# RWKV attention and gated MLP on one core: joint transposing DMAs, and a new order of the work

## The chip, the cores and the metric

The kernel runs on one core of a Trainium2 chip. The metric is device time in microseconds, the median of repeated executions. The engines in the text are TensorE (PE; its weight loads are shown as PEld), VectorE (DVE), ScalarE (ACT), GpSimd (POOL) and SyncE (SP), which issues most of the DMAs. Each runs its own instructions in order and waits for the others through semaphores. A DMA that SP issues is carried out by 16 DMA engines, which all queues share.

## The reference

Inputs r, k, v have shape (4, 8, 768, 48): batch, heads, time, head size. A recurrence over time with a decay w and a bonus u per head gives y; y, with its heads side by side, is the 3072 x 384 input of an MLP with 2048 hidden units and a smooth gate.

```python
for t in range(S):
    cur = einsum('bhd,bhe->bhde', u * k[t], v[t])
    y[t] = einsum('bhd,bhde->bhe', r[t], state + cur)
    state = w * state + einsum('bhd,bhe->bhde', k[t], v[t])
x = y.transpose(0, 2, 1, 3).reshape(B * S, H * D)
h = x @ w_in
g = where(h >= 1, h, where(h <= -1, 0, (h + 1) ** 2 / 4))
out = g @ w_out
```

## The kernel before

The time axis is cut into 6 chunks of 128 steps. A *unit* is one chunk of one batch entry (128 tokens, 8 heads), numbered n; a *group* g is two units, so there are 24 units in 12 groups. Names below are those of the code and, shortened, of the profile.

For each group SP loads R, K and V (L364, L438): 384 KB each, group 0's R and K in two halves. R is scaled by powers of the decay into Rs (L383) and K into Ks (L385), in bf16 and padded from 48 to 64 columns a head. KU = K times u (L387), RKU = R times KU (L389), its sums over a head `diag` (L411), and V2 = V times diag (L416), the bonus term. These products run on GpSimd; in the first three groups (`FLEX`) they may run on VectorE.

Attention of a unit needs scaled R and K turned, so that the head's 48 columns lie on partitions. For groups 0 to 4 (`TDMA` = 5) TensorE turns them: T, eight matmuls against an identity matrix (L462), then a copy TT from PSUM to SBUF by ScalarE or VectorE (L248). From group 5 on SP issues two transposing DMAs per group (L546), one into RT and one into KT. Then come A (L473), its masked copy AT on VectorE (L478), Y from the state and from AT times V (L495, L500), and y = Y + V2 (L507). Sp (L485), Tm (L515), the decay of the state on GpSimd (L520) and its bf16 copy `state_bf` carry the recurrence to the next chunk.

For the MLP y must be turned as well. In groups 0 to 2 (`XDMA` = 3) TensorE does it (X, L528) with a copy to xT; from group 3 on SP issues one transposing DMA per unit (L569), which writes the unit's half of the group's tile xT. mm1 (L602) is four blocks of 12 matmuls with 256 columns per group (in group 0 in halves of 128 columns). Its result passes ScalarE twice (relu L610, square L615) and VectorE once (gate, L620), then mm2 (L651), four blocks of 4 matmuls per unit. The output is copied from PSUM and stored by SP (L666).

The weights are loaded by GpSimd's queue, four transfers of w_in (L320) and four of w_out (L326); the first of each waits for a load of R or K (L314). While the MLP of group 0 has not filled PSUM, gaps on TensorE are filled with identity matmuls, named `warm` (L679).

The order of all this is set by a planner in the kernel. Each operation is declared with `op`: the engines that may run it, with a cost and a delay to its result, a key, what it needs, and the tile slots it takes and frees. A loop then picks, again and again, the operation that can start earliest by these costs (within 0.25 us, the lowest key), and emits it. The table `TUNE` adds an amount to the key by kind and group ('m' is groups 4 to 9), and `ONLY` fixes an operation that has two engines to one of them (0 is the first named). For the products of the first groups 0 is GpSimd and 1 is VectorE; for TT, o and xT 0 is ScalarE and 1 is VectorE. So a changed cost, a changed key and a changed slot count all change the order of every engine's instructions, SP's queue among them. The number of identity matmuls in a gap is worked out from the planner's own idea of how long TensorE will be free.

Of the kernel before, what the change touches and what calls it, by code (L numbers as in the profile page):

```python
# [10 lines left out]
BF16 = mybir.dt.bfloat16  # L11
# [12 lines left out]
def kernel(  # L24
# [86 lines left out]
    Rs = [const.tile([P, UNITS * H, HP], BF16, name="Rs", tag=f"Rs{i}") for i in range(NB)]  # L111
    Ks = [const.tile([P, UNITS * H, HP], BF16, name="Ks", tag=f"Ks{i}") for i in range(NB)]
    for i in range(NB):
        nc.vector.memset(Rs[i][:, :, D:], 0.0)
        nc.vector.memset(Ks[i][:, :, D:], 0.0)
# [31 lines left out]
    FLEX, XDMA, TDMA, VCAST = 3, 3, 5, 12  # L147

    def shift(what, g):
# [17 lines left out]
        'Wdn': {0: -9.14},  # L167
        'Wup': {0: 1.93},
        'X': {0: 0.79, 1: -2.24, 2: -4.04},
        'Y': {0: -0.05, 3: 3.62, 10: 0.23, 11: -1.39, 'm': -2.74},  # L170
        'decay': {2: 0.48, 3: -11.42, 'm': -2.78},
        'exps': {0: 7.52},
        'gate': {0: 20.08, 1: 8.66, 2: -1.81, 3: -14.22, 10: 0.46, 'm': -3.69},
        'load': {0: -2.22, 1: 2.92, 2: 1.11, 11: 5.77, 'm': 11.7},
        'lw': {0: 3.06},
        'lw_row': {0: -3.75},
# [6 lines left out]
        'u_bc': {0: 6.26},  # L183
        'u_row': {'m': -2.41},
        'usum': {0: -0.67, 1: 19.78, 2: 1.23, 3: -1.67, 10: -0.52, 11: 1.53, 'm': -1.65},
        'wCm': {0: 9.26},
        'w_in': {0: -0.2, 1: -1.68, 2: -0.05, 3: 2.64},
        'w_in!': {0: -5.6, 1: 36.74, 2: 2.76, 3: -7.13},
        'w_out': {0: 0.06, 1: -8.78, 2: 4.51, 3: -1.32},
        'w_out!': {1: -0.28, 2: -2.83, 3: 4.56},  # L190
        'w_power': {0: 0.75},
        'w_row': {0: 3.3},
        'w_take': {0: 5.37},
        'wc': {0: 5.72},
        'xT': {0: 9.53, 1: -3.07, 2: 0.34, 3: -1.67, 10: 0.36, 11: 5.32, 'm': -2.7},
        'y': {0: -3.24, 1: 0.72, 2: 1.77, 3: -1.94, 10: -14.8, 11: 4.13, 'm': -3.61},
# [97 lines left out]
    op("w_row", (("NET", 0.0, 3.4),), -99, None)  # L294
    op("u_row4", (("NET", 0.0, 4.4),), -99, None)
    op("lw_row", (("ACT", 0.52, 0.05),), -98, lw_ln, ["w_row"])
    op("lw", (("PE", 1.3, 0.17),), -98, lw_mm, ["lw_row"], [("bank", "lw")], ["lw"])
    op("wc", (("PE", 0.6, 0.17),), -99, w_mm, ["w_row"], [("bank", "wc")], ["wc"])
# [4 lines left out]
    op("w_take", (("DVE", 0.15, 0.08),), -95, w_take, ["wc"], [], ["wc"])  # L303
# [7 lines left out]
    for i in range(max(NW, NO)):  # L311
# [23 lines left out]
        k_in = -70 + i  # L335
        k_out = -1 + i * 0.1 + shift("w_out", i)
        op(f"w_in{i}!", (("POOL", 0.78 + 0.2 * (i in GATE_IN), 1.5),), k_in, w_in_go, after(GATE_IN, i, "w_in"), [], [GATE_IN[i][:2]] if i in GATE_IN else [])
        op(f"w_in{i}", (("SWD", 2.5, 1.35),), k_in, None, [f"w_in{i}!"])
        op(f"w_out{i}!", (("POOL", 0.78 + 0.2 * (i in GATE_OUT), 1.5),), k_out, w_out_go, after(GATE_OUT, i, "w_out"), [], [GATE_OUT[i][:2]] if i in GATE_OUT else [])
        op(f"w_out{i}", (("SWD", 10.6 / NO, 1.35),), k_out, None, [f"w_out{i}!"])  # L340

# [463 lines left out]
```

## Time and profile before

| | |
|---|---|
| median of 3 runs | 183.79 us (183.52 to 184.97) |
| profiled execution | 183.7 us |
| its span in the profile | 181.9 us |
| mean granted TensorE clock | 1.0 |
| matmuls | 1850, of them 182 identity matmuls `warm`, 80 of T, 18 of X |
| transposing DMAs | 32: 18 of y, 7 of R, 7 of K |
| moved by DMA | 27.75 MB, mean 153 GB/s |

The span is shorter than the device time because launch and end lie around it. The profile gives, for each engine, the busy time and its share of the span; groups of instructions by line with their mean duration; a timeline of instructions with start, duration and, in brackets, the idle time before and what ended it; a list of waits; and tables by stretch of time. A line `34.17 2.78 PE L602 MATMUL ... x24` means that 24 matmuls of line 602 began at 34.17 us and the last of them ended 2.78 us later. Matmuls overlap in the pipeline, so the distance from one start to the next says more of their cost than the mean duration does.

### The profile page before, as it was taken

How to read it: one execution, taken by the hardware profiler on the slowest of the kernel's cores; microseconds unless marked ns; L12 is line 12 of the kernel's file. 1: busy time of each engine (PE TensorE's matmuls, PEld its weight loads, DVE VectorE, ACT ScalarE, POOL GpSimd, SP SyncE). 2: the span in 40 equal slices, each digit the busy share in tenths (PEclk: the TensorE clock that was granted, in tenths of full speed). 3: DMA queues.
4: the chain of work that ended last, by engine and by line, in shares of the span. 5: the costliest groups of instructions: out<-in, count | busy, mean ns of one | idle time of the engine just before them, and what ended most of it. 6: DMA issues, size and time to landing. Idle time of an engine off the chain costs nothing.

```text
span 181.9 us, 4539 instructions
## 1 busy us (share of the span) xinstructions
PE 171.7 (94%) x1850; PEld 129.7 (71%) x1850; DVE 140.2 (77%) x207; ACT 133.8 (74%) x169; POOL 111.6 (61%) x88
## 2 busy tenths in 40 slices
PE   5999999969999999999998999999899999999992
PEld 4897888747778787587876677767667777777761
DVE  6977499599998879789986888768687998754360
ACT  5455896678767978668986987786977798774762
POOL 2793553029999998979939949898859551000000
PEclk9999999999999999999999999999999999999999
DMA  6999999999997599998989999889798822101032
GB/s 123 189 214 188 212 199 186 176 208 182 193 192 162 96 218 196 141 215 180 147 151 168 178 200 183 162 179 206 142 183 108 193 83 65 22 4 43 0 130 86
DMA packets 103806, 27.75 MB, mean 153 GB/s; under 512 B 97125, under 2 KB 103786, under 8 KB 103786
## 3 DMA queue, kind: packets, MB, share of 16 engines
q1 hardware_dynamic: 100064, 24.32, 75.5%
q0 software_dynamic: 3712, 3.15, 10.7%
q8 instruction: 14, 0.23, 0.6%
q14 instruction: 6, 0.05, 0.1%
q10 hardware_dynamic: 10, 0.01, 0.0%
HBM read 20.45 MB, written 4.72 MB: 138 GB/s over the span
## 4 chain that ended last, share of the span: by engine, by line
PE 41%; DMA 17%; POOL 14%; SPq 13%; DVE 7%; issue 3%; ACT 3%; DVEq 0%; ACTq 0%; POOLq 0%
PE op L651 18%; PE hp L602 17%; DMA K<-in_k_dram 14%; SPq L364 8%; POOL RKU L389 4%; POOL state L520 3%; DVE gt L620 3%; POOL Ks L385 3%; SPq L438 3%; POOL KU L387 3%; DMA R<-in_r_dram 3%; PE A L473 2%; ACT sq L615 2%; SPq L546 1%; PE T L462 1%
## 5 line engine op out<-in xcount | busy, mean ns | idle before, releaser
L620 DVE SCALAR_TENSOR_TENSOR gt<-sq,hp 128x1024 bf16<-128x1024 f32 (+1 forms) x52 | 58.7, 1134 | 25.5 <-ACT sq L615 25.1
L602 PE MATMUL hp<-xT,w_in_sb 128*128 128x256 bf16 (+1 forms) x624 | 71.7, 264 | 1.8 <-DVE gt L620 1.0
L651 PE MATMUL op<-w_out_sb,gt 128*128 128x384 bf16 x384 | 72.3, 326 | 0.1
L602 PEld LDWEIGHTS <-w_in_sb 128*128 128x128 bf16 x624 | 57.1, 98 | 14.1 <-issue 3.4
L610 ACT ACTIVATE pt<-hp 128x1024 f32<-128x1024 f32 (+1 forms) x52 | 49.6, 954 | 23.5 <-PE hp L602 23.4
L615 ACT ACTIVATE sq<-pt 128x1024 f32<-128x1024 f32 (+1 forms) x52 | 51.6, 992 | 1.1
L651 PEld LDWEIGHTS <-gt 128*128 128x128 bf16 x384 | 34.6, 97 | 18.7 <-DVE gt L620 0.4
L478 DVE TENSOR_TENSOR AT<-A,umask 128x512 bf16<-128x512 f32 x48 | 30.9, 682 | 3.7 <-PE A L473 3.7
L416 POOL TENSOR_TENSOR V<-V,diag 128x768 f32<-128x768 bf16 (+1 forms) x13 | 17.9, 1378 | 16.9 <-DVE diag L411 13.7
L383 POOL TENSOR_TENSOR Rs<-R,Wup 128x768 bf16<-128x768 f32 (+1 forms) x12 | 20.4, 1702 | 5.3 <-DMA R<-in_r_dram 5.0
L520 POOL TENSOR_TENSOR state<-Tm,wCm 128x384 f32<-128x384 f32 x16 | 16.0, 1004 | 5.3 <-DVE Tm L515 5.1
L389 POOL TENSOR_TENSOR RKU<-R,KU 128x768 f32<-128x768 f32 x10 | 18.1, 1819 | 1.4 <-DVE KU L387 1.2
L385 POOL TENSOR_TENSOR Ks<-K,Wdn 128x768 bf16<-128x768 f32 x9 | 16.4, 1825 | 0.9 <-PE hp L602 0.5
L387 POOL TENSOR_TENSOR KU<-K,u_bc 128x768 f32<-128x768 f32 x9 | 16.4, 1828 | 0.0
L679 PE MATMUL warm<-ident 128*128 128x128 bf16 x182 | 14.6, 242 | 1.5 <-POOL ident masks.py:199 1.5
L679 PEld LDWEIGHTS <-ident 128*128 128x128 bf16 x182 | 12.8, 110 | 2.8 <-POOL ident masks.py:199 1.5
L507 DVE TENSOR_TENSOR y<-Y,V 128x384 bf16<-128x384 f32 x24 | 13.1, 551 | 0.8 <-issue 0.2
L248 ACT CAST state_bf<-state 128x384 bf16<-128x384 f32 x20 | 9.8, 506 | 5.1 <-POOL state L520 3.9
L500 PE MATMUL Y<-V,AT 128*128 128x48 bf16 x192 | 11.4, 183 | 1.1 <-ACT V L248 0.9
L248 ACT CAST V<-VF 128x768 bf16<-128x768 f32 x12 | 9.9, 828 | 3.2 <-DMA VF<-in_v_dram 3.1
L411 DVE TENSOR_REDUCE diag<-RKU 128x16 f32<-128x768 f32 (+1 forms) x13 | 11.3, 881 | 1.0 <-POOL RKU L389 1.0
L248 ACT COPY o_sb<-op 128x384 f32<-128x384 f32 x16 | 7.6, 474 | 5.8 <-PE op L651 5.8
(63 smaller groups left out, 127.4 us busy)
## 6 DMA issues: line engine op xcount, KB each, us to landing
VF<-in_v_dram SPq DMA_DIRECT2D x12, 384.0 KB, 5.5
out_dram<-o_sb SPq DMA_DIRECT2D x24, 192.0 KB, 2.3
R<-in_r_dram SPq DMA_DIRECT2D x11, 384.0 KB, 4.6
K<-in_k_dram SPq DMA_DIRECT2D x11, 384.0 KB, 6.0
w_in_sb<-in_moe_w_in_dram POOLq DMA_DIRECT2D x4, 384.0 KB, 9.3
w_out_sb<-in_moe_w_out_dram POOLq DMA_DIRECT2D x4, 384.0 KB, 9.2
R<-in_r_dram SPq DMA_DIRECT2D x2, 192.0 KB, 3.4
K<-in_k_dram SPq DMA_DIRECT2D x2, 192.0 KB, 3.8
```

The source lines that it names most:

```text
L248: nc.scalar.copy(out, in_) if e == "ACT" else engines[e].tensor_copy(out, in_)
L385: engines[e].tensor_mul(part(K_s)[:, :, :, :D], part(K), rep(Wdn, j1 - j0))
L387: engines[e].tensor_mul(part(tiles["KU", g]), part(K), rep(u_row, j1 - j0))
L389: engines[e].tensor_mul(part(tiles["RKU", g]), part(R), part(tiles["KU", g]))
L478: nc.vector.tensor_mul(tiles["AT", n][:, i], tiles["A", n][i], umask.unsqueeze(1).to_broadcast([P, NP, P]))
L520: nc.gpsimd.tensor_mul(states[b], tiles.pop(("Tm", n)), wCm)
L602: nc.tensor.matmul(hp[:, f - f0, cols], w_in_sb[:, i, n0 : n0 + P], tiles["xT", g][:, i, cols], start=(i == 0), stop=(i == nK - 1), skip_g ...
L610: nc.scalar.activation(tiles["pt", g, q][:, f0:f1], tiles["hp", g, q, x], AF.Relu, bias=0.5, scale=0.5)
L615: nc.scalar.activation(tiles["sq", g, q][:, f0:f1], tiles["pt", g, q][:, f0:f1], AF.Square, bias=0.0)
L620: nc.vector.scalar_tensor_tensor(out=tiles["gt", g, q][:, f0:f1], in0=tiles["sq", g, q][:, f0:f1], scalar=1.0, in1=tiles["hp", g, q, x], o ...
L651: nc.tensor.matmul(tiles["op", g, j], tiles["gt", g, q][:, f, j * P : (j + 1) * P], w_out_sb[:, n, :], start=(n == 0), stop=(n == nF - 1),)
L679: nc.tensor.matmul(tiles["warm"][:, :P], ident, ident, start=True, stop=True, skip_group_check=True)
```

## The change

- Scaled R and scaled K of a group now lie in one tile `RKs`, and from group 3 on (`TDMA` = 3) one transposing DMA of 2048 columns turns both into one tile `RKT`. So T and TT remain in groups 0 to 2 alone: 48 identity transposes in place of 80.
- y of both units of a group lies in one tile, and from group 3 on one transposing DMA of 768 columns turns it, after the second unit's y. The tile xT has the unit ahead of the other axes, so mm1's moving operand is two runs of 128 columns.
- Fewer identity matmuls are put into a gap.
- The planner's costs, delays and starting times are changed, and with them `TUNE` and `ONLY`: a new order on every engine.

```diff
-    Rs = [const.tile([P, UNITS * H, HP], BF16, name="Rs", tag=f"Rs{i}") for i in range(NB)]
-    Ks = [const.tile([P, UNITS * H, HP], BF16, name="Ks", tag=f"Ks{i}") for i in range(NB)]
+    RKs = [const.tile([P, 2, UNITS * H, HP], BF16, name="RKs", tag=f"RKs{i}") for i in range(NB)]
...
-    FLEX, XDMA, TDMA, VCAST = 3, 3, 5, 12
+    FLEX, XDMA, TDMA, VCAST = 3, 3, 3, 12
...
-        'TT': {0: 9.21, 1: -23.33, 2: -0.34, 3: 1.52, 'm': 2.52},
+        'TT': {0: 0.32, 1: 0.37, 2: -0.63},
...
-        'relu': {0: 3.23, 1: 6.02, 2: 2.2, 3: 6.37, 10: 4.68, 11: 2.86, 'm': 1.79},
+        'relu': {0: 8.78, 1: -0.14, 2: 2.61, 10: 54.94, 11: 39.14, 'm': 38.93},
...
-        'w_in!': {0: -5.6, 1: 36.74, 2: 2.76, 3: -7.13},
+        'w_in!': {0: -0.14, 1: -5.34, 2: 72.0, 3: -0.28},
...
     ONLY = {
-        'KU': {2: 1},
-        'Ks': {0: 1, 1: 1},
-        'RKU': {1: 0},
-        'Rs': {0: 0},
-        'TT': {0: 0, 1: 0, 2: 1},
-        'V2': {0: 0, 1: 0, 2: 0},
-        'o': {0: 0, 1: 1, 2: 0, 3: 0},
-        'xT': {0: 0, 1: 0, 2: 0},
+        'KU': {1: 1, 2: 0},
+        'Ks': {0: 1, 1: 0, 2: 1},
+        'RKU': {0: 0, 1: 0, 2: 0},
+        'Rs': {2: 0},
+        'TT': {0: 0},
+        'V2': {1: 1},
+        'o': {0: 1, 1: 0, 2: 0, 3: 0},
+        'w_power': {0: 1},
+        'xT': {0: 0},
     }
...
-                op(f"load {what}{tag}", (("DMA", (0.95 if g == 0 else 1.05) * n, 1.35),), ...
+                op(f"load {what}{tag}", (("DMA", 1.05 * n, 1.95),), ...
...
             def y_out(e, g=g, j=j, n=n):
-                y = tiles["y", n] = att.tile([P, DM], BF16, name="y", tag="y", bufs=3)
+                if j == 0:
+                    tiles["y", g] = att.tile([P, UNITS, DM], BF16, name="y", tag="y", bufs=2)
...
+                    def t_dma(e, g=g):
+                        t = tiles["RKT", g] = att.tile([P, 2 * UNITS * NP, P], BF16, name="RKT", tag="RKT", bufs=2)
+                        nc.sync.dma_start_transpose(out=t, in_=RKs[g % NB].rearrange("p i h d -> p (i h d)"))
+
+                    op(f"RKT{g}", (("DMA", 1.9, 2.7),), ka - 1.5, t_dma, [f"Rs{part}", f"Ks{part}"],
+                       [("RKT", ("RKT", g))], [("RKT", g), ("Rs", g), ("Ks", g)])
...
+            def x_dma(e, g=g):
+                tiles["xT", g] = moe.tile([P, UNITS, nK, P], BF16, name="xT", tag="xT", bufs=3)
+                nc.sync.dma_start_transpose(
+                    out=tiles["xT", g].rearrange("p u k t -> p (u k) t"), in_=tiles["y", g].rearrange("p u c -> p (u c)")
+                )
...
-            else:
-                op(f"xT{n}", (("DMA", 1.2, 2.0),), ka + 3, x_dma, [f"y{n}"], [] if j else [("xT", ("xT", g))], [("y", n), ("xT", g)])
+            elif j == UNITS - 1:
+                op(f"xT{n}", (("DMA", 1.36, 1.6),), ka + 3, x_dma, [f"y{n - y}" for y in range(UNITS)], [("xT", ("xT", g))], [("y", g), ("xT", g)])
...
-                                hp[:, f - f0, cols], w_in_sb[:, i, n0 : n0 + P], tiles["xT", g][:, i, cols], ...
+                                hp[:, f - f0, cols], w_in_sb[:, i, n0 : n0 + P], tiles["xT", g][:, us, i, :], ...
...
-    free = {"POOL": 3.9, "DVE": 3.0, "DMA": 1.55}
+    free = {"POOL": 2.2, "DVE": 3.0, "DMA": 0.7, "ACT": 3.2}
...
-                fill(int((spare - 0.1) / (0.11 if s < 7 else 0.06)))
+                fill(int((spare - 0.25) / (0.1 if s < 10 else 0.075)))
```

More of the change, by code (lines that the diff above doesn't have):

```diff
@@ L196 @@
-        'y': {0: -3.24, 1: 0.72, 2: 1.77, 3: -1.94, 10: -14.8, 11: 4.13, 'm': -3.61},
[13 rows of a table added]
+        'Wdn': {0: -0.87},
+        'Wup': {0: -0.29},
+        'X': {0: -2.09, 1: -0.1, 2: -3.29},
+        'Y': {0: 1.7, 1: -3.71, 2: -2.99, 3: 0.9, 10: 0.22, 11: 0.58, 'm': -30.29},
+        'decay': {2: 15.51, 'm': 9.96},
+        'exps': {0: -1.81},
[9 rows of a table added]
+        'u_bc': {0: -2.42},
+        'u_row': {'m': 0.19},
+        'usum': {0: 1.34, 1: 34.65, 2: 3.89, 3: 2.95, 10: 8.26, 11: 6.02, 'm': -8.84},
+        'wCm': {0: 0.25},
@@ L370, in product @@
                 if ("scaled", g) not in tiles:
-                    tiles["scaled", g] = (Rs[g % NB], Ks[g % NB])
+                    tiles["scaled", g] = [RKs[g % NB][:, i] for i in range(2)]
                 if i == 2 and j0 == 0:
@@ L540 @@
             else:
-                tt = f"KT{g}"
+                tt = f"RKT{g}"
                 if j == 0:
-                    for i in range(2):
-                        def t_dma(e, g=g, i=i):
-                            t = tiles["RK"[i] + "T", g] = att.tile([P, UNITS * NP, P], BF16, name="RK"[i] + "T", tag="RK"[i] + "T", bufs=2)
-                            nc.sync.dma_start_transpose(out=t, in_=tiles["scaled", g][i].rearrange("p h d -> p (h d)"))
-                        w_ = "RK"[i] + "s"
-                        op(f"{'RK'[i]}T{g}", (("DMA", 1.4, 3.0),), ka - 2 + i, t_dma, [f"{w_}{part}"] + ([f"RT{g}"] if i else []),
-                           [("RK"[i] + "T", ("RK"[i] + "T", g))], [("RK"[i] + "T", g), (w_, g)])
+                    def t_dma(e, g=g):
[3 more added lines that the diff above has]
+                       [("RKT", ("RKT", g))], [("RKT", g), ("Rs", g), ("Ks", g)])
             op(f"A{n}", (("PE", 0.34, 0.17),), ka + 1, a_mm, [tt], [("bank", ("A0", n)), ("bank", ("A1", n))], [("A0", n), ("A1", n)] + tt_tiles)
@@ L669 @@
             op(f"o {o}", where, k2 + 0.2 + shift("o", g), o_out, [f"mm2 {o}{nQ - 1}"], [("o_sb", ("o_sb", o))], [("op", o), ("o_sb", o)])
-            op(f"out {o}", (("DMA", 0.45, 2.0),), k2 + 0.3, store, [f"o {o}"], [], [("o_sb", o)])
+            op(f"out {o}", (("DMA", 0.62, 2.0),), k2 + 0.3, store, [f"o {o}"], [], [("o_sb", o)])
     WARM = (2.2, 99.0)
```

85 lines of the change are left out of this document (34 added, 51 removed), and 37 rows, old and new, of the table TUNE.

## The prediction

> **What bounds it now.** I read the page's busy shares first, then TensorE's timeline, then the rows of the engines that feed it. TensorE (PE) is the bound.
>
> ```profile
> PE 171.7 (94%) x1850; PEld 129.7 (71%) x1850; DVE 140.2 (77%) x207; ACT 133.8 (74%) x169; POOL 111.6 (61%) x88
> ```
>
> Busy can flatter, so I counted PE's work by start-to-start times in its timeline, from 34.17 us (first full mm1) to 178.6 (end of the last mm2): 44 mm1 blocks at 1.31 = 57.6, 91 mm2 blocks at 0.65 = 59.2, 20 units of A at 0.33 and Y at 0.37 = 14.0, 16 of Sp at 0.17 = 2.7, 6 of T at 0.45 = 2.7, 2 of X = 0.3. That is 136.5 of 144.4 us: only some 8 us of waits and bubbles. What leaves PE in this stretch leaves the time; what leaves another engine does not, unless PE waits for it. Ahead of 34 us PE idles or runs identity matmuls, so there the chain decides. Its rows (start, duration, engine, line):
>
> ```profile
> 5.38 4.60 PE L679 MATMUL warm<-ident 128*128 128x128 bf16 x48
> 9.82 0.39 PE L462 MATMUL T<-ident,Rs 128*128 128x128 bf16 x4
> ...
> 10.26 1.78 PE L679 MATMUL warm<-ident 128*128 128x128 bf16 x29
> ...
> 12.31 0.40 PE L462 MATMUL T<-ident,Rs 128*128 128x128 bf16 x4
> ...
> 36.79 0.39 PE L462 MATMUL T<-ident,Rs 128*128 128x128 bf16 x4
> 38.60 0.40 PE L462 MATMUL T<-ident,Ks 128*128 128x128 bf16 x4 [1.43 <-DVE Ks L385]
> ...
> 45.58 0.39 PE L462 MATMUL T<-ident,Rs 128*128 128x128 bf16 x4
> 45.81 0.39 PE L462 MATMUL T<-ident,Ks 128*128 128x128 bf16 x4
> 46.03 0.21 PE L495 MATMUL Y<-state_bf,TT 128*128 128x96 bf16 x1
> ```
>
> The reader sees three things: a block of 48 identity matmuls that holds the first T until 9.82; one real wait of 1.43 us in group 2; and a T that costs 46.03 - 45.58 = 0.45 us.
>
> **T of groups 3 and 4 goes to the DMA queue.** Units 6 to 9 (T at 45.58, 48.98, 61.07, 67.55) lose 0.45 us each: **-1.8 us**, all in the PE-bound stretch. Their four TT copies (0.68 each on VectorE) go too; 2.7 us that cost nothing directly, as PE does not wait for that engine there. What is late next is the transfer. ScaledK of group 3 ends at 44.62 on POOL and A of unit 6 starts at 47.80. These rows give issue to landing:
>
> ```profile
> xT<-y SPq DMA_TRANSPOSE x18, 2.4
> RT<-Rs SPq DMA_TRANSPOSE x7, 3.7
> KT<-Ks SPq DMA_TRANSPOSE x7, 4.1
> ```
>
> The joint transfer of 2048 columns is no row. Below, 4.1 (one half, last in line); above, 8.2 (two in a row). I take 5, near the lower end, since K loads of 384 KB, close to its 512 KB, have a median of 6.0 with a queue ahead of them. Then A starts near 49.6, 1.8 us late. Cover: unit 6's AT is done at 50.98 but its Y starts at 55.90, 4.9 us of other PE work. At 8.2 it is 5.0 late and the cover is just gone, about 0.1 us. Group 4: scaled K ends at 53.28, A starts at 62.92; covered by either end. In groups 5 to 11 the joint transfer starts when the K half starts now; 1 us more to landing is covered by 2.8 us (group 7: issue 88.63, A at 95.53) or more except in group 9 (issue 116.87, A at 121.74: 0.8). **0**, ends 0 and +0.5.
>
> **Queue.** SP issues 18 transposes in place of 32 (7 x 2 + 18). Each holds SP 1.18 to 1.27 us; a wide one between 1.2 and 2.5. Behind a waiting transpose stand loads and stores; SP's waits for POOL's products are 8.1 + 4.0 + 2.2 us. A joint transfer waits once per group, but R no longer leaves before K is ready. No PE wait is put down to SP, so 0, ends -0.5 and +0.5.
>
> **DMA engines.** R and K of two groups add 4 x 128 x 1024 x 2 B = 1.05 MB. The transfers run here (us, busy by engine, clock, DMA share, GB/s):
>
> ```profile
> 40.00:50.00 10.00, 10.00 (x124) 7.31 (x123) 9.68 (x15) 8.16 (x11) 9.92 (x6) 1.00 1.05 188
> 50.00:60.00 10.00, 10.00 (x112) 7.83 (x111) 9.14 (x15) 7.07 (x8) 9.69 (x7) 1.00 1.05 166
> ```
>
> At their mean of 177 GB/s it is 5.9 us of transfer time. Within them some microseconds move little (17 GB/s at 45, 52 at 59), so part fits; I take 0, ends 0 and +5.9. The Trainium skill (Advanced Engine Details and Errata, X-Bar Transpose) holds a transpose to be as fast as a plain transfer and expects 350 to 400 GB/s; by that the addition would be an estimated 2.8 us. Rows of loads and transposes here stay at or below 267 GB/s in any microsecond I looked at, so the bound stays at 5.9.
>
> **One transfer for y.** It starts with the second y, as the later of two does now, with 768 columns for 384. Between 2.4 and 3.7 us: 3.2 by columns, 0.8 later. Cover: group 3's second transfer is issued at 59.87, lands near 62.3, and mm1 starts at 63.91; group 11: 159.6 against 162.78. **0**, ends 0 and +0.8 in a group without cover. mm1's moving operand becomes two runs of 128 columns. Six 128-column matmuls take 0.33 us (15.80 to 16.13), so twelve halves 0.66, against 0.655 for six whole ones: 0, upper end 528 x 1 ns = 0.5.
>
> **The head.** Scaled R of unit 0 is ready at 8.48, but the block of 48 holds T to 9.82: 1.3 us. Scaled R of unit 1 stands on POOL behind three weight transfers:
>
> ```profile
> 7.30 1.18 POOL L383 TENSOR_TENSOR Rs<-R,Wup 128x384 bf16<-128x384 f32 x1
> 8.44 2.34 POOL L320 DMA_DIRECT2D w_in_sb<-in_moe_w_in_dram  x3
> 10.80 1.01 POOL L383 TENSOR_TENSOR Rs<-R,Wup 128x384 bf16<-128x384 f32 x1
> ```
>
> The diff pushes the third of the four weight transfers (and the fourth, which follows it) far back, no longer fixes group 0's scaled R to POOL, and takes more margin in sizing identity blocks (0.25 for 0.1). So both T can come 1.3 us or more earlier. How much reaches the end is limited at group 2, whose K lands at 35.7:
>
> ```profile
> 35.73 0.96 DVE L387 TENSOR_TENSOR KU<-K,u_bc 128x768 f32<-128x768 f32 x1 [1.96 <-DMA K<-in_k_dram]
> 36.72 0.96 DVE L389 TENSOR_TENSOR RKU<-R,KU 128x768 f32<-128x768 f32 x1
> 37.60 0.95 DVE L385 TENSOR_TENSOR Ks<-K,Wdn 128x768 bf16<-128x768 f32 x1
> ```
>
> The diff pins KU and RKU of group 2 to POOL and Ks to VectorE, so Ks can come first, 1.87 us earlier, and the wait of 1.43 goes. The two gains are one, for the earlier head needs group 2 to be earlier as well: I take **-1.4 us** for both. Ends: 0, if POOL (1.82 us each, and behind them group 3's products, from 41.0 on) gives it back; -2.4 (1.3 and 1.1 more, if K lands earlier too).
>
> Fewer identity matmuls have a price: the block at 5.38 runs at 4.60/48 = 96 ns each, the one at 10.26 at 61, though the clock column reads 1.00 in both. The slow stretch may last longer. The Trainium skill (TensorE: Matmul & The Clock Gate, Part 1) says activity over a window of some 3.4 us opens the clock and an idle window closes it; the two spacings agree in kind.
>
> **Sum.** The profiled execution took 183.7 us, 1.8 around its span of 181.9, and stands 0.1 under the median 183.79. 183.7 - 1.8 - 1.4 = **180.5 us**, 1.8% under the median. About 1% is what a measurement of this kernel tells from no change.
>
> **Rivals.**
> - *Transfers become the bound* (slower). Loads wait behind the 1.05 MB in groups 3 and 4. For it: POOL already waits 5.0 us in all for R, 0.58 of them at 68.6, and POOL is 93 to 99% busy from 40 to 70. Against it: the empty microseconds and 14 fewer transposes. It decides once the delay passes the 0.6 us that POOL idles at 68: then scaled R, Y and mm1 all slip. Price +5.9 with nothing hidden: 186.4; with half of it hidden, 183.5. Slower by over 1% means from 185.6 up: 0.20, of which 0.15 above 185.9.
> - *The new order opens waits as large as what it saves.* PE's recorded waits from 40 us on are only 2.5 us, so there is more to lose than to win; a repeat of the 1.43 in two places and no head gain: 183.7 - 1.8 + 0.4 = 182.3 to 183.7. Chance 0.16.
> - *Cold matmuls in the head.* Should the rule just named bite, T, A, Y, X and the first mm1 (0.45 + 0.33 + 0.20 + 0.17 + 0.33 = 1.5 us on a unit's path) double: 182.0, so within 1%. The mechanism in rows is the 96 ns against 61 above. Chance 0.06.
> - *More from the head:* -2.4 there, and 1 of the 2.5 us of later waits: 178.5. Chance 0.13.
> - *Forecast:* 179.5 to 181.9, chance 0.45.
>
> **Numbers.** Faster by over 1%: 0.45 + 0.13 = 0.58. Within 1%: 0.16 + 0.06 = 0.22. Slower: 0.20. The range is 178.0 to 185.9: it takes in the forecast, the two middle rivals and most of the larger gain, and leaves out 0.15 above (the transfer rival nearly in full) and some 0.04 below.
>
> **What would show it.** Right: 48 T matmuls in place of 80, none after group 2; no idle of a microsecond ahead of group 2's T; the first T before 9 us; the first full mm1 near 33 us; PE without waits over 0.5 us from 40 to 70. Wrong: POOL's waits for R well above 5.0 us, A or Y with waits for the joint transfer, mm1 above 1.31 us a block, or identity blocks that still end after T's inputs are ready. The weakest step is the head, where the order can't be followed operation by operation.

## The result and the profile after

The changed kernel took **187.89 us** (median, 187.37 to 188.62); the kernel before took 183.66 beside it (183.43 to 184.97). The ratio is 1.0249 with a 95% interval of 1.0203 to 1.0295: slower by 2.5%, or some 4.5 us. The forecast was 180.5, and the range ended at 185.9. The profiled execution took 188.62 us. Medians are of all executions of a kernel; ratios leave out those that took over 1.5% more than its fastest one.

The top of the page of the changed kernel: its span, the busy times and the granted clock in 40 slices.

```profile
span 186.8 us, 4227 instructions
...
PE 168.1 (90%) x1724; PEld 125.5 (67%) x1724; DVE 140.1 (75%) x200; ACT 133.7 (72%) x169; POOL 115.8 (62%) x88
...
PEclk9999966999999999999999999999999999999999
```

TensorE has 126 matmuls and 3.6 us of busy time less than before, and the span is 4.9 us longer: more of its time is idle. And two slices, near 23 to 33 us, show a clock of 0.6 that the kernel before does not have. TensorE's timeline in the head:

```profile
7.17 0.63 PE L460 MATMUL T<-ident,RKs 128*128 128x128 bf16 x4
...
15.20 0.34 PE L527 MATMUL X<-ident,y 128*128 128x128 bf16 x3 [1.12 <-DVE y L506]
...
19.77 1.11 PE L678 MATMUL warm<-ident 128*128 128x128 bf16 x17
23.15 0.49 PE L601 MATMUL hp<-xT,w_in_sb 128*128 128x128 bf16 x6 [2.27 <-DVE gt L619]
23.48 0.39 PE L460 MATMUL T<-ident,RKs 128*128 128x128 bf16 x4
25.18 1.46 PE L460 MATMUL T<-ident,RKs 128*128 128x128 bf16 x12 [1.31 <-POOL RKs L383]
...
39.68 2.57 PE L601 MATMUL hp<-xT,w_in_sb 128*128 128x256 bf16 x22
```

The first T comes at 7.17 in place of 9.82, as forecast, but the first X comes at 15.20 where it was 14.89. Then two waits, 2.27 and 1.31 us, stand close together, and the first full mm1 starts at 39.68 where it was 34.17 and was forecast near 33. The same stretch by windows of 2 us (busy by engine, then clock, DMA share, GB/s):

```profile
24.00:26.00 2.00, 0.82 (x8) 0.83 (x9) 0.18 (x1) 0.00 (x0) 2.00 (x3) 0.64 1.00 149
26.00:28.00 2.00, 2.00 (x23) 1.61 (x22) 1.25 (x3) 1.33 (x2) 2.00 (x3) 0.50 1.26 185
28.00:30.00 2.00, 2.00 (x24) 1.61 (x22) 2.00 (x4) 1.53 (x4) 2.00 (x2) 0.50 1.31 234
30.00:32.00 2.00, 2.00 (x36) 1.96 (x35) 1.25 (x3) 1.35 (x3) 2.00 (x2) 0.66 1.25 179
```

Behind the waits TensorE counts as wholly busy, at half its clock. A slice that reads "PE 2.00" can so hide half of its time; the clock column has to be read with it.

What the two waits are made of stands in the timelines of VectorE, ScalarE and POOL:

```profile
21.54 0.96 DVE L385 TENSOR_TENSOR KU<-K,u_bc 128x768 f32<-128x768 f32 x1 [3.73 <-DMA K<-in_k_dram]
22.42 1.28 DVE L619 SCALAR_TENSOR_TENSOR gt<-sq,hp 128x512 bf16<-128x512 f32 x2
```

```profile
19.93 0.63 ACT L614 ACTIVATE sq<-pt 128x512 f32<-128x512 f32 x1
```

```profile
21.64 0.90 POOL L312 COPY gone<-K 1x1 f32<-1x1 f32 x1 [7.38 <-DMA K<-in_k_dram]
22.48 0.80 POOL L324 DMA_DIRECT2D w_out_sb<-in_moe_w_out_dram  x1
23.31 1.81 POOL L383 TENSOR_TENSOR RKs<-K,Wdn 128x768 bf16<-128x768 f32 x1
```

The square that the first gate needs is ready at 20.56, but VectorE, which works in order, stands at KU of group 1 and waits for K until 21.5; the gate follows at 22.42. Scaled K of group 1 was on VectorE before (21.81 to 22.76). Now it stands on POOL behind a weight transfer and ends at 25.12. K of group 1 is itself later: POOL's first read of it starts at 21.64, where it started at 19.81 before. No run separates this from the order.

Later, between 38 and 110 us, the waits of the changed kernel name transfers (in total, times, longest):

```profile
POOL RKs L381 <- DMA R<-in_r_dram: 6.3, 2, 6.2
...
PEld L601 <- DMA xT<-y: 2.0, 2, 1.2
...
ACT V L246 <- DMA VF<-in_v_dram: 1.9, 2, 1.0
```

In that stretch POOL waited 2.9 us for R before, and TensorE for no xT. The 6.2 us for R are no doing of the added transfers: that wait ended at 40.81, and the first joint transfer was issued at 45.12. Nor did it delay the product, scaled R of group 3, which started at 41.01 before. The landings of the two joint transfers:

```profile
RKT<-RKs SPq DMA_TRANSPOSE x9, 5.2
xT<-y SPq DMA_TRANSPOSE x9, 3.5
```

**Where the time went.** I counted TensorE's lost time by the start-to-start durations of the prediction: the time gone, less the work of all matmuls started by then, with identity matmuls counted as nothing. The work fell from 150.4 to 148.6 us, the 1.8 that was forecast. The lost time rose from 21.8 to 24.6 by 40 us, and from 28.2 to 34.5 by the last matmul: +2.8 in the head, +3.5 behind it (+2.4 from 40 to 60, +0.9 from 60 to 90, +0.2 after that). TensorE's recorded waits behind 40 us grew from 2.4 to 5.3 us. Those from 40 to 60 (2.1) name gates, a y and a copy of xT, which are VectorE's and ScalarE's work; none names a load or a joint transfer.

### The profile page after: what moved, and what is told of

It is laid out like the page before. It is cut to its first block, busy times and chain, and to the rows that moved or that the text cites. A ratio compares the mean times of both kernels' runs of the same rounds, so it can differ in the third digit from the quotient of the medians.

```text
span 186.8 us, 4227 instructions
## 1 busy us (share of the span) xinstructions
PE 168.1 (90%) x1724; PEld 125.5 (67%) x1724; DVE 140.1 (75%) x200; ACT 133.7 (72%) x169; POOL 115.8 (62%) x88
## 4 chain that ended last, share of the span: by engine, by line
PE 39%; DMA 28%; ACT 12%; DVE 7%; SPq 5%; POOL 4%; issue 3%; ACTq 0%; DVEq 0%; POOLq 0%
PE hp L601 18%; PE op L650 17%; DMA K<-in_k_dram 8%; DMA VF<-in_v_dram 8%; DMA w_out_sb<-in_moe_w_out_dram 7%; DMA xT<-y 5%; ACT sq L614 5%; ACT pt L609 4%; DVE gt L619 3%; SPq L362 3%; DVE AT L476 1%; PE A L471 1%; POOL w_out_sb L324 1%; ACT V L246 1%; DVE V L414 1%
## 5 line engine op out<-in xcount | busy, mean ns | idle before, releaser
L601 PE MATMUL hp<-xT,w_in_sb 128*128 128x256 bf16 (+1 forms) x624 | 72.7, 268 | 5.7 <-DVE gt L619 3.8
L601 PEld LDWEIGHTS <-w_in_sb 128*128 128x128 bf16 x624 | 58.1, 100 | 17.8 <-issue 6.2
L609 ACT ACTIVATE pt<-hp 128x1024 f32<-128x1024 f32 (+1 forms) x52 | 49.6, 954 | 19.3 <-PE hp L601 19.1
L381 POOL TENSOR_TENSOR RKs<-R,Wup 128x768 bf16<-128x768 f32 x11 | 20.4, 1854 | 6.4 <-DMA R<-in_r_dram 6.3
L387 POOL TENSOR_TENSOR RKU<-R,KU 128x768 f32<-128x768 f32 (+1 forms) x13 | 22.6, 1740 | 0.7
L383 POOL TENSOR_TENSOR RKs<-K,Wdn 128x768 bf16<-128x768 f32 x10 | 18.2, 1822 | 3.8 <-DMA K<-in_k_dram 3.4
L414 POOL TENSOR_TENSOR V<-V,diag 128x768 f32<-128x768 bf16 x9 | 13.3, 1476 | 8.7 <-DVE diag L409 8.5
L385 POOL TENSOR_TENSOR KU<-K,u_bc 128x768 f32<-128x768 f32 x10 | 18.3, 1828 | 0.0
L498 PEld LDWEIGHTS <-AT 128*128 128x128 bf16 x192 | 9.9, 97 | 2.1 <-DVE AT L476 1.5
L678 PE MATMUL warm<-ident 128*128 128x128 bf16 x88 | 8.0, 247 | 1.5 <-POOL ident masks.py:199 1.5
```

What stands on the lines that cost most here:

```text
L381: engines[e].tensor_mul(part(R_s)[:, :, :, :D], part(R), rep(Wup, j1 - j0))
L383: engines[e].tensor_mul(part(K_s)[:, :, :, :D], part(K), rep(Wdn, j1 - j0))
L385: engines[e].tensor_mul(part(tiles["KU", g]), part(K), rep(u_row, j1 - j0))
L387: engines[e].tensor_mul(part(tiles["RKU", g]), part(R), part(tiles["KU", g]))
L498: nc.tensor.matmul(Y[:, 2 * p + i, :], AT[:, i, p, :], V[:, j * H + 2 * p + i, :], start=(c == 0), stop=True, skip_group_check=True,)
L601: nc.tensor.matmul(hp[:, f - f0, cols], w_in_sb[:, i, n0 : n0 + P], tiles["xT", g][:, us, i, :], start=(i == 0), stop=(i == nK - 1), skip_ ...
```

## The experiments

Eighteen runs in four groups. Kernels sent together ran on one chip beside the kernel before, whose median lay between 183.19 and 184.03; so ratios are compared, and a difference in microseconds is that of two ratios times 183.66. Its interval is worked out from the two intervals as independent.

### Whose numbers set the order

The planner's order depends on its numbers (costs, margins, the tables of shifts and engines), which the change replaced together with the structure. The first run is the changed structure with all numbers of before, the second the structure of before with the changed numbers:

```diff
-    free = {"POOL": 2.2, "DVE": 3.0, "DMA": 0.7, "ACT": 3.2}     # first run; the second the other way round
+    free = {"POOL": 3.9, "DVE": 3.0, "DMA": 1.55}
...
-                op(f"load {what}{tag}", (("DMA", 1.05 * n, 1.95),), ...
+                op(f"load {what}{tag}", (("DMA", (0.95 if g == 0 else 1.05) * n, 1.35),), ...
```

> The changed kernel's structure (joint transposes of R with K from group 3 on, joint transpose of y) with every planner number of the kernel before: costs, delays, starting times, TUNE, ONLY, identity matmuls. Order theory (the loss lies in the new order of the first 40 us): the first full mm1 comes near 34.2 us as before, 182 identity matmuls, and the time is 182 us (183.7 less the 1.8 of T), at most 184. Structure theory (the joint transfers make PE wait): at least 186 us, with the loss behind the first full mm1.

> The counterpart: the structure of the kernel before (T on TensorE for groups 0 to 4, one transposing DMA each for R, K and each y) with every planner number of the changed kernel. Order theory: the first full mm1 near 39.7 us and about 189 us (187.9 and the T that comes back, 1.8). Structure theory: back to about 184 us.

190.85 us, ratio 1.0416 (1.0357 to 1.0475), and 191.10, 1.0424 (1.0359 to 1.0489): both are 4% slower than before, and slower than the change itself. The first has its first full mm1 at 34.02 like the kernel before, and then 10.2 us of recorded TensorE waits, where the kernel before has 3.8; the second has it at 39.72 like the changed kernel. So the late first mm1 goes with the numbers, not with the structure. But a re-planned kernel mixes the parts: numbers searched for one structure cost 4% in the other. The runs that follow therefore keep an order instruction by instruction and change one thing in it.

### The head

**Identity blocks.** The formula of before in the changed kernel, same order; then the changed formula, but 2.5 times as many from the planner's 18 us on:

```diff
-                fill(int((spare - 0.25) / (0.1 if s < 10 else 0.075)))
+                fill(int((spare - 0.1) / (0.11 if s < 7 else 0.06)))                             # first run
+                fill(int((spare - 0.25) / (0.1 if s < 10 else 0.075 if s < 18 else 0.03)))       # second run
```

> The changed kernel with only the sizing of the identity blocks of before; the order of all other work is untouched. Clock theory (fewer identity matmuls let the TensorE clock fall to 0.5 between 24.7 and 31 us, and that makes the head late): clock near 1.0 there and about 184 to 185 us. Queue theory (VectorE's and POOL's order in the head makes PE wait, and the low clock only follows): the waits before 23 and 25 us stay and less than 2 us come back, 186 to 188.

> The changed kernel with two and a half times as many identity matmuls in each gap from the planner's 18 us on, the order untouched. Clock theory: no low clock in the head, 184 to 185 us. Queue theory: clock near 1.0, but the first full mm1 still past 37 us, 186 to 187.5.

The first: 185.35 us, 1.0131 (1.0053 to 1.0208), clock 0.998; 2.2 us (0.5 to 3.8) of the change's loss is gone. How, its trace does not show: the profiled execution took 187.04, the longest of the four, and its first full mm1 starts at 40.50, later than the 39.68 of the change. The second: 188.12, 1.0255 (1.0157 to 1.0352), no gain. Its timeline and windows:

```profile
19.76 2.51 PE L678 MATMUL warm<-ident 128*128 128x128 bf16 x42
23.26 0.49 PE L601 MATMUL hp<-xT,w_in_sb 128*128 128x128 bf16 x6 [0.99 <-DVE gt L619]
...
25.29 0.95 PE L460 MATMUL T<-ident,RKs 128*128 128x128 bf16 x12 [1.26 <-POOL RKs L383]
```

```profile
26.00:28.00 2.00, 2.00 (x23) 1.51 (x20) 1.56 (x3) 1.72 (x3) 2.00 (x3) 0.50 1.29 229
28.00:30.00 2.00, 2.00 (x35) 1.70 (x34) 1.99 (x4) 1.55 (x3) 2.00 (x2) 0.67 1.35 213
```

Between 22.27 and 25.29 the identity block is over, the rest are small pieces, and the clock still falls, for 3.4 us. But the clock does not decide the time of this run: of its other executions one had a mean clock of 1.0 and took 188.53 us, one 0.998 and 186.20.

**The order on VectorE and POOL.** The changed kernel's order with two instructions moved: scaled K of group 1 to VectorE, and it and KU behind the two gates that were ready. Then the same with the identity formula of before:

```diff
+    for name, behind in [("Ks1.0", "gate (0, 0)1"), ("KU1.0", "Ks1.0")]:      # Ks1.0 on VectorE
+        x = emit.pop(next(i for i, x in enumerate(emit) if x[0] == name))
+        emit.insert(1 + next(i for i, x in enumerate(emit) if x[0] == behind), x)
```

> The changed kernel with its order kept but for two instructions: the product of K for group 1 with the decay moves from POOL, where it stands behind a weight transfer, to VectorE, and both K products of group 1 stand behind the two gates that were ready at 20.6 us. Queue theory: PE's waits of 2.27 and 1.31 us at 23 and 25 us go, the clock stays at 1.0, and 2 to 3 us come back: 185 to 186. Clock theory: with the same few identity matmuls the clock still falls, and less than 1 us comes back.

> The changed kernel with both repairs of its first 40 us: the identity blocks sized as before, and group 1's scaled K on VectorE, with both K products of group 1 behind the two gates. If the two losses add (2.5 us from the identity matmuls, 1.1 from the queues): 184.3. If both only undo the same low clock: 185.3, as with the identity matmuls alone. Below 182.5 only if nothing was lost behind 60 us.

The first: 186.81 us, 1.0188 (1.0158 to 1.0218), 1.1 us (0.1 to 2.1) back. The two waits in TensorE's timeline are now

```profile
21.30 0.49 PE L601 MATMUL hp<-xT,w_in_sb 128*128 128x128 bf16 x6 [0.45 <-DVE gt L619]
...
23.32 0.84 PE L460 MATMUL T<-ident,RKs 128*128 128x128 bf16 x12 [1.30 <-DVE RKs L383]
```

and the granted clock of this execution is 1.0 in every slice, though identity matmuls are as few as in the change. But the other three executions had a mean clock of 0.988 to 0.991, like the change's (0.982 to 0.996), and took 186.75 to 187.43 us, where the profiled one took 186.63. So it is not shown that the waits alone lower the clock, nor that the clock is what came back.

What else moved is in POOL's and TensorE's rows, first of the change, then of this run:

```profile
25.06 2.29 POOL L324 DMA_DIRECT2D w_out_sb<-in_moe_w_out_dram  x3
...
39.04 0.81 PE L650 MATMUL op<-w_out_sb,gt 128*128 128x384 bf16 x4 [0.37 <-DMA w_out_sb<-in_moe_w_out_dram]
```

```profile
37.08 0.81 PE L650 MATMUL op<-w_out_sb,gt 128*128 128x384 bf16 x4 [0.57 <-DMA w_out_sb<-in_moe_w_out_dram]
37.73 2.78 PE L601 MATMUL hp<-xT,w_in_sb 128*128 128x256 bf16 x24
```

The last transfer of w_out waits on POOL for K of group 1 and for its scaled K. It is issued at 26.59 and lands at 39.00 (25.47 and 35.18 in the kernel before, where no TensorE wait names it); an mm2 block waits for it, and the first full mm1 stands behind that block. With scaled K gone from POOL it is issued at 24.77 and lands at 37.04, and the first full mm1 comes at 37.73. The low clock is not on this path: the run with split transfers (below) has the head of the change, but in its profiled execution half as much low clock, 3.4 us in place of 6.8. Its lost time at 32 us is 1.0 less, its wait for the last w_out is 0.61, and its first full mm1 starts at 39.69, as in the change.

The second run: 184.20, 1.0034 (0.9990 to 1.0079). The two repairs add up within their intervals: together they give back 3.9 us (2.8 to 5.1) of the change's 4.5.

**Does an earlier T gain anything?** The kernel before with the changed identity formula alone (114 identity matmuls for 182):

```diff
-                fill(int((spare - 0.1) / (0.11 if s < 7 else 0.06)))
+                fill(int((spare - 0.25) / (0.1 if s < 10 else 0.075)))
```

> The kernel before with the change's formula for identity blocks alone; the order of all other instructions is kept, 114 identity matmuls in place of 182. By the prediction's head step (the first block of 48 holds T for 1.3 us): up to 1.3 us faster, 182.4. By the clock theory (what replaces identity work is idle time, and the clock falls): 184 to 186.7, with rows of the granted clock under 0.9 between 8 and 36 us. If neither: 183.3 to 184.

184.14 us, 0.9993 (0.9959 to 1.0028): neither theory, no difference. Its timeline:

```profile
8.54 0.40 PE L462 MATMUL T<-ident,Rs 128*128 128x128 bf16 x4
...
15.00 0.50 PE L602 MATMUL hp<-xT,w_in_sb 128*128 128x128 bf16 x6 [0.28 <-ACT xT L248]
...
17.18 0.51 PE L602 MATMUL hp<-xT,w_in_sb 128*128 128x128 bf16 x6 [1.12 <-DMA w_in_sb<-in_moe_w_in_dram]
```

T is 1.28 us earlier and the first mm1 0.80 (15.80 before); then mm1 waits for its weights and for the gates, and the first full mm1 starts at 34.36 against 34.17. What the block of 48 held up was not late.

**Group 2's products.** Two runs on the kernel before with one transfer for y (below): scaled K of group 2 ahead of the two products for V, on VectorE; and the same with the first identity block cut short (160 for 182):

```diff
+    for name, behind in [("KU2.0", "Ks2.0"), ("RKU2.0", "KU2.0")]:            # both runs
...
-                fill(int((spare - 0.1) / (0.11 if s < 7 else 0.06)))
+                fill(int((spare - 0.1) / (0.11 if s < 10 else 0.06)))         # second run
```

> The kernel before's order with the joint transfer of y (182.6 us) and one more move: VectorE's scaled K of group 2 stands ahead of KU and RKU, not behind them. My prediction's step: the wait of T for it (0.9 to 1.4 us near 38.6) goes, 181.2 to 181.8. Rival: K of group 2 lands at 35.7 and PE is bound by the gates there, so the wait only moves: 182.4 to 182.9.

> The kernel before in its order with one transfer for y and scaled K of group 2 ahead of the other two products (182.33 us in the earlier run), and the identity blocks up to 10 us of the planner's clock sized with 0.11 us each as the first ones are: 160 in place of 182. Head step: the first T starts near 8.5 in place of 9.82 and some of that reaches the end, 181.0 to 182.0. Rival: the rest of the head (VectorE's and POOL's products and the loads of group 1) sets the first gates, so the same as the earlier run, 182.1 to 182.6.

182.33 us, 0.9914 (0.9880 to 0.9947), and 182.14, 0.9902 (0.9864 to 0.9939). Both beat both kernels; but against the run with one transfer for y alone (0.9944) the moved products bring 0.3%, and the shorter block another 0.1%, neither beyond the intervals. In the first, T no longer waits; two rows on, A does:

```profile
37.70 0.61 PE L472 MATMUL T<-ident,RKs 128*128 128x128 bf16 x8
...
40.31 0.40 PE L485 MATMUL A<-TT 48*128 48x128 bf16 x8 [0.70 <-DVE TT L248]
```

### The structure, in the order of before

**One transfer for y**, and, in another run, **T of groups 3 and 4 as one joint transfer each**, issued where T of the group's first unit stood; then **all parts together** in that order:

```diff
-                nc.sync.dma_start_transpose(out=tiles["xT", g][:, :, j * P : (j + 1) * P], in_=tiles["y", n])
+                if j == UNITS - 1:                                              # first run
+                    nc.sync.dma_start_transpose(out=..both units of xT.., in_=..both units of y..)
...
             def t_in(e, bank, g=g, j=j, n=n):
+                if g >= 3:                                                      # second run
+                    if j == 0:
+                        nc.sync.dma_start_transpose(out=..RKT.., in_=..scaled R and K of the group..)
+                    return
```

> The kernel before with its order of every engine kept, instruction by instruction; only the two transposing DMAs of a group's y become one, issued where the second stood. Theory A (the new transfers cost nothing by themselves, the new order loses): 183 to 184 us, the same as before. Theory B (the joint transfer of y lands 1.1 us later than the single one, 3.5 against 2.4, and PE waits for it): waits of mm1 for xT in several groups and 185 us or more.

> The kernel before with its order kept, but the T matmuls and TT copies of units 6 to 9 are left to one joint transposing DMA for each of groups 3 and 4, issued where the first T stood (R and K of groups 5 to 11 keep their two DMAs). PE loses 1.8 us of work. Theory A: A of unit 6 stands at 47.8 us in PE's order and its transfer lands near 50, so PE waits about 2 us once, group 4 does not wait: 183.5 to 184. My prediction's account (0 for lateness): 181.9. Theory B (loads behind the joint transfers come late): waits of POOL for R and K grow by 2 us or more and the time is 185 or more.

> The whole structure of the change (joint y, joint R with K from group 3 on, no T after group 2) in the kernel before's order, instruction by instruction. Theory A: 182 to 184. Theory B (each joint transpose of R and K holds SP for some 3.5 us, in place of 1.25 for a single one, and what stands behind it is late): 186 or more, with the waits after 60 us.

The first: **182.63 us, 0.9944 (0.9914 to 0.9974)**: one transfer for y is a gain of 1.0 us, and nothing waits for xT longer. The second: 189.55, 1.0336 (1.0300 to 1.0372). The third: 189.67, 1.0340 (1.0297 to 1.0382). TensorE's timeline and windows in the second:

```profile
45.68 1.46 PE L675 MATMUL op<-w_out_sb,gt 128*128 128x384 bf16 x8
49.84 0.40 PE L485 MATMUL A<-RKT 48*128 48x128 bf16 x8 [2.70 <-DMA RKT<-RKs]
...
52.20 2.67 PE L626 MATMUL hp<-xT,w_in_sb 128*128 128x256 bf16 x12
```

```profile
48.00:50.00 2.00, 0.16 (x6) 0.16 (x8) 0.00 (x0) 0.59 (x1) 2.00 (x2) 1.00 1.01 216
50.00:52.00 2.00, 2.00 (x19) 1.15 (x16) 1.73 (x3) 0.48 (x1) 0.61 (x2) 0.81 1.07 208
52.00:54.00 2.00, 2.00 (x11) 1.34 (x10) 1.55 (x2) 0.00 (x0) 2.00 (x2) 0.50 1.25 212
```

TensorE takes its instructions in order, so A of unit 6, once late, holds all work behind it; and a wait of 2.70 us is followed by half the clock, so that twelve matmuls of mm1 take 2.67 us where they took 1.31. It happens again at 68.84 (2.82 us): the transfer of group 4 was issued only at 64.37.

**The transfer where it is covered.** All parts in the order of before, but A of unit 6 and its copies behind the next mm1 and gate, and the joint transfer of group 4 behind a load:

```diff
+    for name, behind in [("T8", "loadV5"), ("A6", "mm1 (2, 0)00"), ("AT6.0", "gate (1, 3)0"), ("AT6.1", "AT6.0")]:
```

> All of the change's structure in the kernel before's order, and the transfers of groups 3 and 4 placed for their delay: group 4's is issued behind V's load of group 5 and not behind the transfer of group 3's y, and A of unit 6 with its masked copies stands behind the next mm1 block. Lateness theory (what cost 5.8 us in the two kernels with T by DMA in the old order is A waiting for its transfer in PE's queue, twice 2.8 us, and the low clock after it): no wait for RKT over 1 us, clock 1.0, 181 to 183.5. Bandwidth theory (1.05 MB more and SP held longer make all loads late): the waits for RKT go, but 186 or more remains, with waits for R, K and gates behind 60 us.

185.82 us, 1.0108 (1.0043 to 1.0172), with no wait for the transfer: the lateness was worth 4.3 us (2.8 to 5.7) of the run before. But it is still 1% slower than the kernel before, with T gone from TensorE and no wait for the transfer. That left the question why.

**The joint form.** The changed kernel with each transfer of scaled R and K as two of half the size:

```diff
-                        nc.sync.dma_start_transpose(out=t, in_=RKs[g % NB].rearrange("p i h d -> p (i h d)"))
+                        for i in range(2):
+                            nc.sync.dma_start_transpose(out=t[:, i * UNITS * NP : (i + 1) * UNITS * NP], in_=..RKs[g % NB][:, i]..)
```

> The changed kernel in its own order, each joint transpose of R with K issued as two of 1024 columns at the same place in SP's queue. If the joint form holds SP by itself (3.5 us at the median, against 1.25 each): SP is held 2.5 us for the two, and 186 to 187. If SP is held by what the DMA queues still have to do: the second of the two is held as long, and the time stays at 187.5 to 188.5.

188.55 us, 1.0250 (1.0197 to 1.0304), the same as the change. SP is held 3.92, 3.27, 4.00 and 3.48 us by the first four joint transfers and 3.99, 3.48, 4.43 and 3.47 by the pairs: the form does not matter. Within a pair the second half takes 1.24 to 1.31 us each time; only the first is held.

### What the added transfers cost

Four runs on the kernel with one transfer for y (0.9944), in its order. **T taken out**, with nothing in its place (A and Y of units 6 to 9 read another unit's transposes); **the transfers added**, into a tile that nobody reads, with T still on TensorE; the same place in SP's queue with **the wait but hardly any bytes**; and with **the bytes but no wait**:

```diff
             def t_in(e, bank, g=g, j=j, n=n):
+                if g >= 3: return                                                # first run
...
+                if g >= 3 and j == 0:                                            # the others: out is never read
+                    nc.sync.dma_start_transpose(out=.., in_=..all 2048 columns of scaled R and K..)         # second
+                    nc.sync.dma_start_transpose(out=.., in_=..128 columns of scaled K..)                    # third
+                    nc.sync.dma_start_transpose(out=.., in_=..2048 columns of w_in_sb, long in place..)     # fourth
```

> The same kernel without T and its TT copies for units 6 to 9; A and Y of these units read unit 5's TT, so the transposes of scaled R and K of groups 3 and 4 are left out and those outputs are not the reference's. It measures what taking T off TensorE is worth by itself, with nothing late and nothing added. The prediction's term: 4 x 0.45 = 1.8 us, so 180.8. A rival: that part of PE's time is filled by other waits (VectorE's and POOL's products), so under 0.9 us reaches the end: 181.7 to 182.6.

> The kernel before in its own order, with one transfer per group for y (182.63 us in the earlier run), and beside it one transposing transfer of scaled R and K of groups 3 and 4 (512 KB each, at the place of T of units 6 and 8 in SP's queue) into a tile that nobody reads; T stays on TensorE. It adds the traffic of the change and none of its dependences. Traffic theory (the 1.05 MB costs time whoever reads it): 184.6 us or more, up to the 186.4 of the prediction's rival. Lateness theory (A of the unit waits for its own transfer, and the idle TensorE then runs at half clock): 182.6 to 183.2, with no wait of TensorE over 0.3 us that the earlier run does not have.

> As the run with two transfers that nobody reads (187.88 us), but each transposes only 128 columns of scaled K in place of 2048 columns of R and K: 32 KB for 512 KB. SP still stands at the same two places until scaled K of the group is ready, so the loads behind it still wait, but 94% of the added traffic is gone. Queue theory (SP standing in front of the loads is the cost): 186.5 to 187.9, and VectorE, ScalarE and POOL again wait about 4 us for R and 5 us for V. Traffic theory: 182.6 to 184.

> The complement: the same two transposing transfers of 2048 columns at the same places in SP's queue, but of weights that have long been in place, so that SP never waits for scaled K; all of the 1.05 MB is there. Queue theory: 182.6 to 184. Traffic theory: 186.5 to 188. If both runs lie between (184.5 to 186), each theory has a part.

| run | us | ratio to before | against 0.9944, in us |
|---|---|---|---|
| T taken out | 181.77 | 0.9846 (0.9763 to 0.9930) | -1.8 (-3.4 to -0.2) |
| transfers added | 187.88 | 1.0189 (1.0121 to 1.0257) | +4.5 (3.1 to 5.9) |
| the wait alone | 183.86 | 1.0056 (1.0025 to 1.0087) | +2.1 (1.3 to 2.9) |
| the bytes alone | 185.31 | 1.0148 (1.0086 to 1.0210) | +3.7 (2.5 to 5.0) |

Taking T out is worth the 1.8 us that the row of 0.45 gave, though the interval is wide. Two transfers that nobody reads cost 4.5 us. Of the two theories for that each has a part. The bytes' price is the larger, though the intervals touch; the single prices sum to 5.8, which the intervals do not tell from the pair's 4.5. The waits between 38 and 110 us, first of the kernel with one transfer for y, then with the transfers added, then with the bytes alone, then with the wait alone:

```profile
POOL RKs L385 <- DMA R<-in_r_dram: 0.8, 2, 0.6
...
ACT V L248 <- DMA VF<-in_v_dram: 0.6, 1, 0.6
```

```profile
ACT V L248 <- DMA VF<-in_v_dram: 5.5, 4, 2.3
...
POOL RKs L385 <- DMA R<-in_r_dram: 4.3, 4, 2.2
```

```profile
ACT V L248 <- DMA VF<-in_v_dram: 4.3, 4, 2.0
...
POOL RKs L385 <- DMA R<-in_r_dram: 3.5, 2, 2.0
```

```profile
POOL RKs L385 <- DMA R<-in_r_dram: 3.0, 3, 1.3
...
ACT V L248 <- DMA VF<-in_v_dram: 1.3, 2, 0.9
```

The loads come late: issued on SP after the first added transfer, R of the next group leaves at 50.72 in place of 47.80, and R after the second at 68.18 in place of 64.01. ScalarE then waits for V and POOL for R, and what they feed reaches TensorE late. All three added-transfer runs show a granted clock of 1.0, so this is not the clock.

**The sum.** One transfer for y (-1.0), T off TensorE (-1.8) and the added transfers (+4.5) make +1.7; the run with all parts and no wait for the transfer measured +2.0. The changed kernel with its head mended is at +0.6, so its searched order may hide about a microsecond more than the order of before does (1.4, with an interval of -0.1 to 2.8). The head's 3.9 is the difference of that +0.6 to the 4.5, so it adds up by definition.

## Why the prediction was wrong

- **"T of groups 3 and 4 goes to the DMA queue", -1.8.** The size was right (148.6 against 150.4 us of work; 1.8 by the run without T, with a wide interval). The delay was right too: A of unit 6 was worked out for 49.6 and came at 49.84 and 49.64 in the two runs with the transfer. The cover was argued wrongly for the order of before: 4.9 us between AT and Y of unit 6 is slack for Y, but A itself stands in TensorE's queue, and everything behind it waits (2.70 us, and half the clock after it). Group 4, "covered by either end", waited 2.82: its transfer left at 64.37, not when scaled K was ready. In the changed kernel the new order puts A of unit 6 at 56.48, in place of 47.80, and no TensorE wait names the transfer.
- **"DMA engines", 0 with an end of +5.9.** In the order of before this step failed: 3.7 us for the bytes alone, 4.5 with the wait. For the changed kernel's own loss behind 40 us it is not shown, since its largest part, from 40 to 60, names no transfer. The evidence was in the two rows that I showed: a DMA share of 1.05 in both. I set it aside for a few microseconds with little traffic. The Trainium skill (Advanced Engine Details and Errata, X-Bar Transpose) holds a transpose to be as fast as a plain transfer and expects 350 to 400 GB/s, which gave an estimated 2.8 us. That lies inside the 2.5 to 5.0 measured for the bytes alone, and my 5.9 by the mean rate outside. Either price was nearer than the 0 that I took.
- **"Queue", 0 with ends of 0.5.** Also too small: SP standing at a transfer until scaled K is ready costs 2.1 us by itself, since the loads of the next groups are behind it. The reading was too narrow: "1.18 to 1.27 us" are the shorter ones of the 32 transposes before, others held SP up to 2.57. And a joint transfer holds SP 3.48 us in the median of the changed kernel, not 1.2 to 2.5, for one as for two of half the size.
- **"One transfer for y", 0.** Right in its mechanism (landing 3.5 us against the 3.2 worked out, 2.8 in the run with it alone), and better than 0: -1.0 us. No run shows why it gains.
- **"The head", -1.4.** Failed, with the largest size: about +3.9. The first T came 2.65 us earlier, but the unit's path to X goes over VectorE, which the new order also gave scaled R of group 0 (two products of 0.54 and 0.56 us) and V's factor (0.93 and 1.24), POOL's before; y of unit 0 starts at 14.60 in place of 14.28. An earlier T alone, in the old order, brought nothing that could be measured (0.9993), and Ks of group 2 first brought 0.3%, inside the interval. One reading was wrong: the third and fourth weight transfers were not pushed far back. They left at 9.67 and 10.47, in place of 9.24 and 10.01, for a key decides only among operations that can start at about the same time. What I had not followed is the order of group 1: KU ahead of ready gates, scaled K behind a weight transfer, and the last w_out transfers behind both. Which of the two repairs' gains comes by which of these stays open, and so does what the identity matmuls do in it.
- **The rivals.** "Transfers become the bound" measured 3.7 to 4.5 us in the order of before, between its half and its full price; I gave it 0.20. "The new order opens waits" is what the rows of the changed kernel show from 40 to 60 us. Its sum was wrong: two more waits of 1.43 without a head gain make 184.8, not at most 183.7. "Cold matmuls in the head" was right that the clock would fall, and wrong in place: not the first blocks but 24 to 32 us, where 8 us at a mean clock of 0.57 are worth at most 3.4 us. What it cost is less: half of it cost nothing up to the first full mm1, which waited for w_out, and of the change's four executions the one with a mean clock of 0.996 took 187.69, those at 0.982 took 188.10 and 188.62. The Trainium skill (TensorE: Matmul & The Clock Gate, Part 1) has an idle window of some 3.4 us close the clock. The rows agree that idle time goes before the fall, and it can be shorter: single waits of 2.70, 2.11 and 1.75 us. They give no limit, for after one of 1.79 in the run with all parts the clock stayed at 1.0.

What I had listed as signs came out mixed: 48 T matmuls and no wait ahead of group 2's T, yes; the first T before 9 us, yes; the first full mm1 near 33, no (39.68); TensorE without waits over 0.5 us from 40 to 70, no (0.69, 0.99); POOL's waits for R well above 5.0 in all, hardly (6.3, but 6.2 of it in one, ahead of the first joint transfer).

Open stays how much of the changed kernel's own loss behind the head is bytes and how much its order; the prices of the transfers were measured in the order of before.

## What to carry to other kernels

Where a change adds a transfer in windows with a DMA share near 1.0, do not price it at nothing: here the loads behind it paid 3.7 to 4.5 us, though nobody read it. Look for the engine that waits for the next load, not for its reader. An early start is worth only what the next late input leaves of it; follow a unit through every engine to the first full block before booking it, and ask when the last weights land. A low clock beside a late block is not yet its cause: look for an execution without it. And where an order is searched anew with a change, keep one order fixed and change one thing in it to find out what a part is worth; tables searched for another structure cost 4% here and price no part.

## What the runs showed of the hardware

- **The clock falls in mid-kernel.** After an idle 2.70 us at 47 us into the kernel the granted clock was 0.81 and then 0.50 (1.31 us of mm1 took 2.67). In every profiled execution here a stretch of half clock ahead of TensorE's last matmul lasted 3.4 us, or 6.8 in the change.
- **It can differ between executions of one kernel.** The run with T taken out has one wait of 2.11 us ahead of group 2's T; its profiled execution shows a clock of 0.50 at 42 to 44 us and took 183.75 us, its three others at a clock of 1.0 took 180.57 to 182.05. The run with the first identity block cut short has one of 1.75 us ahead of A; its profiled execution shows 0.50 at 42 to 44 us and took 184.30, its nine others at 0.998 to 1.0 took 181.70 to 182.57.
- **How long SP is held goes with what is queued ahead, hardly with the size.** A joint transfer of 2048 columns held SP 1.4 us with little ahead of it (at 45 us in the order of before) and up to 5.49 us in the changed kernel.
